# Second mixture of a three-stage kernel: each phase's compaction before its neighbours' counts, and its row transposes at a new place in TensorE's order

## The chip, the cores and the metric

The kernel runs on one core of a Trainium2 chip. The metric is the device time in microseconds (us) of one execution, as the median of the runs. In the text, PE is TensorE, DVE is VectorE, ACT is ScalarE, POOL is GpSimd and SP is SyncE.

## The reference

Three stages follow one another. The first is a recurrent attention over 4 batches, 8 heads and 768 steps. Its result, seen as 3072 tokens of 384 numbers, goes through a first mixture of 8 experts and then through a second. Only the second mixture is touched here:

```python
def _moe2_ref(x, w_gate, w1, w2):
    N, D = x.shape                      # 3072, 384
    E = w_gate.shape[1]                 # 8
    cap = N // E                        # 384
    flat = (x @ w_gate).flatten()
    order = np.argsort(-flat)
    assigned = -np.ones(N); counts = np.zeros(E)
    for idx in order:
        tok, e = int(idx) // E, int(idx) % E
        if assigned[tok] >= 0 or counts[e] >= cap:
            continue
        assigned[tok] = e; counts[e] += 1
    for e in range(E):
        mask = assigned == e
        out[mask] = np.maximum(x[mask] @ w1[e], 0.0) @ w2[e]
```

All pairs of token and expert are taken in falling order of their logit. A token goes to the first expert that still has room, and an expert is full at 384 tokens. So the experts fill up one after another, and each of them ends with exactly 384 tokens.

## The kernel before

The attention and the first mixture come first and end at about 539 us of the profiled execution. What follows is the second mixture, in 8 phases, one for each expert in the order in which they fill up. A phase p has these parts.

**The chain** (`chain(p)`) finds which expert fills up next and which tokens it gets. The key of every token is cut into three digits of 10 or 11 bits, and each digit is found in two levels. So a chain has six **counts**. In a count, DVE compares all keys with 46 thresholds (tile `cmp`), PE adds the results up in 12 products (L953, into `pcn`), DVE scales the sums (`xs`), PE adds over partitions (L960), DVE compares with what is still needed (`fl`), PE spreads that (L964), and DVE takes the maximum (`nn`), from which the next count's keys are made. After the sixth count come two more small products (L985 and L1018), and from them the list of free tokens for the next chain (`advance`). Phase 7 has no counts.

**The compaction** (`finish`, that is `place` and `compact`) turns the chosen tokens into a list of 384 row numbers: DVE compares in four parts (`oq`, L1077), PE makes 24 products (L1081, into `pcm`, in four parts of 6), DVE makes the indices `ix`, and POOL issues three indirect DMAs (the **gather**, L1094), each of which fetches 128 rows of the first mixture's output into `x2`.

**The transposes** (`tin`, L1134): for each of three column blocks kt, three products turn the rows (a = 0, 1, 2) into `pX`. ACT and DVE split that into a high and a low part (`x2h`, `x2l`). `pX` has two buffers, so the third block waits until the first has been split.

**The products** (`compute`): 72 products into `pH` (L518 to L520, the first matrix) and 72 into `pY` (the second), 144 a phase, each 128x384. `pH` has two buffers, each free once ACT (`h2h`) and DVE (`h2l`, L515) have read it. `pY` is written three times, for 128 tokens each; ACT scales it (`orow`, L1162) and POOL scatters it to the output (L1163).

**The weights** (`load2`): SP reads the number of the expert (`ei`) and loads four pieces of 768 KB into `stage`; ACT makes the high part `whi` (L1119) and DVE the low part `wlo` (L1120), in 16 pieces a phase.

A scheduler lays out one fixed order of instructions for each engine when the kernel is built. It takes the work in the order in which the code emits it, and what stands in `tc.high_priority(n)` counts as if it had been emitted n places earlier. `tc.issue_after(x)` keeps an instruction behind x in the order. At run time each engine takes its instructions in that order, and one that waits holds up all behind it on its engine. `compute(p)` yields 14 times, u counts the yields, and the loop over u emits the next phase's parts between the products: the chain of p + 1 and its compaction at u = 1 (`UC`), the weights at u = 3 and 11, the transposes at u = 11 (`UT`). The compaction of phases 2 to 7 has half the chain's priority, and the transposes are kept behind the product emitted last.

Of the kernel before, what the change touches and what calls it, by code (L numbers as in the profile page):

```python
# [28 lines left out]
E = 8  # L29
# [11 lines left out]
KS = 46  # L41
# [9 lines left out]
UC = 1  # L51
UT = 11
HC = 1000000
HP2 = HC // 2
HT = 1000
HL = 0
DEF = 2
# [11 lines left out]
H1 = 300  # L69
# [3 lines left out]
IT = 1  # L73
# [8 lines left out]
def tile_kernel(ctx: ExitStack, tc, rd, kd, wd, vd, ud, emb, tau, m1w1, m1w2, m1w2t, wg2, m2w1, m2w2, out):  # L82
    nc = tc.nc
# [11 lines left out]
    def bcast(ap, shape):  # L95
        return ap.to_broadcast(shape)
# [410 lines left out]
    pe = [None]  # L507

    def split_x(pX, n, hi, lo):
        nc.scalar.copy(hi, pX)  # L510
        nc.vector.tensor_sub(lo, pX, hi.bitcast(F32))
# [372 lines left out]
    with tc.tile_pool(name="m2", bufs=2) as mp, tc.tile_pool(name="ps2", bufs=2, space=PSUM) as ps:  # L884
# [4 lines left out]
        def small(shape, name, dt=F32, bufs=None):  # L889
            bufs = bufs or 1 + (name in twin)  # L890
            return ck.tile(shape, dt, name=name, bufs=bufs)

        plan = {}
        oqi = [None]
        pcm = ps.tile([128, 512], F32, name="pcm", bufs=1)

        def chain(p):
# [4 lines left out]
            if not last:  # L902
# [30 lines left out]
                for s in range(3):  # L933
                    for lv in range(2):
                        cmp = cmps[lv]
                        nq = 2 if p == 0 else NQ
                        hj = J // 2 // nq
                        w2 = w.rearrange("p (a b) -> p a b", b=2)
                        c4 = cmp[:, :J * KS].rearrange("p (a k b) -> p a k b", k=KS, b=2)
                        for q in range(nq):  # L940
                            js = slice(q * hj, (q + 1) * hj)
                            nc.vector.tensor_tensor(c4[:, js], bcast(w2[:, js, None, :], [128, hj, KS, 2]),
                                                    bcast((tblB if lv else tblA)[:, None], [128, hj, KS, 2]), op=ALU.is_ge)
                        if lv == 0:
                            w45 = small([128, J], "w45")
                            nc.vector.tensor_scalar(w45, w, float(KW), None, op0=ALU.add)
                            if s < 2:
                                big = small([128, J], "big")
                                nc.vector.scalar_tensor_tensor(big, w, SPLIT, dg[:, s + 1], op0=ALU.mult, op1=ALU.add)
                        o = 16 * lv  # L950
                        px = pcn[:, 48 + o:64 + o]
                        for a in range(J // 2):
                            nc.tensor.matmul(px, cmp[:, 2 * KS * a:2 * KS * a + 128],  # L953
                                             oh[:, 2 * a:2 * a + 2, :].rearrange("p b e -> p (b e)"),
                                             start=(a == 0), stop=(a == J // 2 - 1))
                        xs = small([128, 2, E], "xs", FP16)
                        nc.vector.tensor_tensor(xs, px.rearrange("p (b e) -> p b e", b=2), par16, op=ALU.mult)
                        pa = pcn[:, o:o + 8]
                        for b in range(2):
                            nc.tensor.matmul(pa[:, :E], psum2, xs[:, b], start=(b == 0), stop=(b == 1))  # L960
                        fl = small([KS, E], "fl", BF16)
                        nc.vector.tensor_tensor(fl, pa[:KS, :E], need[:KS], op=ALU.is_ge)
                        pb = pcn[:, o + 8:o + 16]
                        nc.tensor.matmul(pb[:, :E], ones[:KS, :], fl, start=True, stop=True)  # L964
                        nn = small([128, 1], "nn", bufs=4)
                        nc.vector.reduce_max(nn, pb[:, :E], axis=AX.X)
                        if lv == 0:
                            wn = small([128, J], "wb", FP16)
                            nc.vector.scalar_tensor_tensor(wn, bcast(nn, [128, J]), -float(KW), w45, op0=ALU.mult, op1=ALU.add)
                            w = wn  # L970
                            t1 = small([128, 1], "t1")
                            nc.vector.tensor_scalar(t1, nn, KW * SPLIT, -(KW + 1) * SPLIT, op0=ALU.mult, op1=ALU.add)
                        elif s < 2:
                            t4 = small([128, 1], "t4")
                            nc.vector.tensor_scalar(t4, nn, SPLIT, t1, op0=ALU.mult, op1=ALU.add)
                            wc = small([128, J], "wc")
                            nc.vector.tensor_scalar(wc, big, t4, SPLIT, op0=ALU.subtract, op1=ALU.min)
                            w = small([128, J], "w", FP16)
                            nc.vector.tensor_scalar(w, wc, -1.0, None, op0=ALU.max)
# [70 lines left out]
            def finish():  # L1050
                place()
                compact(p, slot)

            plan[p]["finish"] = finish
            if p == 0:
                with tc.high_priority(HC + 1000):
                    finish()
            if not last:
                advance()

# [65 lines left out]
        def tin(p):  # L1126
            d = plan[p]
            xh = d["xh"] = mp.tile([128, KT, CAP], F32R, name="x2h")
            xl = d["xl"] = mp.tile([128, KT, CAP], F32R, name="x2l")
            for kt in range(KT):  # L1130
                pX = ps.tile([128, CAP], F32, name="pX", bufs=2)
                for a in range(3):
                  with tc.issue_after(pe[0].ins) if IT and p else ExitStack():
                    nc.tensor.transpose(pX[:, a * 128:(a + 1) * 128], d["xr"][:, a, kt * 128:(kt + 1) * 128], ident)  # L1134
                split_x(pX, CAP, xh[:, kt, :], xl[:, kt, :])

# [33 lines left out]
        def hp(n, f, *a):  # L1170
            with tc.high_priority(n) if n else ExitStack():
                f(*a)

        hp(HC, chain, 0)
        load2(0, 0)
        if T0:
            hp(HC, tin, 0)
        if not UW:
            load2(0, 1)
        if not T0:  # L1180
            tin(0)
        for p in range(E):
            more = p + 1 < E
            for u, _ in enumerate(compute(p)):
                if UW and p == 0 and u == UW - 1:
                    load2(0, 1)
                if more:
                    if u == UC:
                        hp(H1 if p == 0 else HC, chain, p + 1)
                        hp(H1 if p == 0 else HP2, plan[p + 1]["finish"])  # L1190
                    if u == U0:
                        hp(HL, load2, p + 1, 0)
                    if u == U1:
                        hp(HL, load2, p + 1, 1)
                    if u == UT:
                        hp(HT, tin, p + 1)
# [51 lines left out]
```

## Time and profile before

| what | value |
|---|---|
| median of 3 runs | 855.87 us (852.36 to 856.16) |
| the profiled execution, its own time | 852.17 us |
| its span, first to last instruction | 850.4 us |
| mean granted clock of TensorE | 0.942 of full |
| busy in the span: PE, DVE, ACT, POOL | 776.8, 554.7, 319.9, 227.9 us |

The span is divided into stretches, and in each the profile gives the busy time of every engine and the clock that TensorE was granted, as a share of 2.4 GHz; there are two levels, 1.0 and 0.5. The work outside the span takes 852.17 - 850.4 = 1.8 us.

### The profile page before, as it was taken

What the parts mean: (1) busy time and instruction counts of PE and PEld (TensorE: products, weight loads), DVE (VectorE), ACT (ScalarE), POOL (GpSimd) and SP (SyncE); (2) the same over time, 40 slices, a digit from 0 to 9 for tenths busy, and PEclk for the clock granted to TensorE, in tenths of its full rate; (3) what the DMA queues carried; (4) which work ended last, traced back from release to release, by engine and by line L of the source; (5) the groups of instructions that cost most, each with busy time, mean ns of one, the idle gap of its engine ahead of it and who ended that gap; (6) DMA issues with size and microseconds to landing.
All of it is one profiled execution on the core that took longest, in us unless ns stands there. A gap on an engine that the chain in (4) does not pass through costs nothing.

```text
span 850.4 us, 14966 instructions
## 1 busy us (share of the span) xinstructions
PE 776.8 (91%) x5484; PEld 681.1 (80%) x5484; DVE 554.7 (65%) x1740; ACT 319.9 (38%) x763; POOL 227.9 (27%) x220
## 2 busy tenths in 40 slices
PE   5898998999989998999989999697979889899997
PEld 3787787888659897998989787485868778789997
DVE  9688899999534355344543546676878778787430
ACT  3334444443323454344443411423323323235431
POOL 4235477853200303203123002302021210112011
PEclk9799899999989999999999999787969979899999
DMA  8567457661253243433523002422323242426300
GB/s 277 167 193 247 137 185 249 189 202 39 66 181 116 102 149 100 158 114 106 184 88 105 5 1 84 150 87 100 124 72 140 80 154 94 145 69 223 122 29 29
DMA packets 39303, 107.66 MB, mean 127 GB/s; under 512 B 6666, under 2 KB 16700, under 8 KB 39228
## 3 DMA queue, kind: packets, MB, share of 16 engines
q1 hardware_dynamic: 32060, 87.71, 31.5%
q0 software_dynamic: 7168, 18.98, 6.3%
q8 instruction: 44, 0.72, 0.3%
q14 instruction: 31, 0.25, 0.1%
HBM read 87.16 MB, written 19.90 MB: 126 GB/s over the span
## 4 chain that ended last, share of the span: by engine, by line
PE 46%; issue 15%; DVE 4%; POOL 2%; DMA 1%; ACT 1%; another core or an unknown queue 1%; ACTq 0%; POOLq 0%; DVEq 0%
PE pY L520 7%; PE pY L518 7%; PE pY L519 6%; PE pH L518 6%; PE pH L519 6%; PE pH L520 6%; PE pO L657 2%; PE pcm L1081 1%; PE pcn L953 1%; DVE wlo L1120 1%; PE pX L624 1%; POOL x L1094 1%; POOL out_dram L1163 1%; PE pX L1134 1%
## 5 line engine op out<-in xcount | busy, mean ns | idle before, releaser
L515 DVE SCALAR_TENSOR_TENSOR hl<-pH,hh 128x416 fp32r<-128x416 f32 x64 | 37.6, 589 | 66.4 <-ACT hh L514 48.5
L518 PE MATMUL pH<-xhi,whi 128*128 128x416 f32 x192 | 72.1, 376 | 9.5 <-DVE hl L515 7.8
L1120 DVE TENSOR_TENSOR wlo<-stage,whi 128x384 fp32r<-128x384 f32 x128 | 68.3, 549 | 6.9 <-ACT whi L1119 6.8
L518 PE MATMUL pH<-x2h,whi 128*128 128x384 f32 x192 | 71.1, 371 | 1.8 <-DVE h2l L515 1.6
L734 POOL DMA_INDIRECT lg<-lr,ids x24 | 23.0, 959 | 179.6 <-DVE lr L659 173.2
L519 PE MATMUL pH<-x2l,whi 128*128 128x384 f32 x192 | 71.1, 371 | 0.0
L520 PE MATMUL pH<-x2h,wlo 128*128 128x384 f32 x192 | 70.1, 365 | 0.0
L1119 ACT CAST whi<-stage 128x384 fp32r<-128x384 f32 x128 | 57.0, 511 | 32.7 <-PE pH L519 19.3
L520 PE MATMUL pH<-xhi,wlo 128*128 128x416 f32 x192 | 69.0, 359 | 0.0
L519 PE MATMUL pH<-xlo,whi 128*128 128x416 f32 x192 | 68.6, 357 | 0.0
L518 PE MATMUL pY<-whi,h2h 128*128 128x384 f32 x192 | 67.7, 353 | 0.0
L520 PE MATMUL pY<-whi,h2l 128*128 128x384 f32 x192 | 67.7, 355 | 0.0
L1163 POOL DMA_INDIRECT out_dram<-orow,ix x24 | 24.3, 1015 | 159.3 <-ACT orow L1162 144.6
L519 PE MATMUL pY<-wlo,h2h 128*128 128x384 f32 x192 | 66.9, 350 | 0.0
L514 ACT ACTIVATE h2h<-pH 128x384 fp32r<-128x384 f32 x64 | 31.4, 490 | 93.8 <-PE pH L520 92.7
L188 DVE TENSOR_TENSOR wlo<-stage,whi 128x512 fp32r<-128x512 f32 x78 | 48.3, 684 | 24.8 <-ACT whi L187 24.8
L187 ACT CAST whi<-stage 128x512 fp32r<-128x512 f32 (+1 forms) x90 | 51.9, 647 | 31.5 <-PE pY L519 23.0
L520 PE MATMUL pY<-hh,wlo 128*128 128x416 f32 x168 | 60.5, 360 | 0.0
L518 PE MATMUL pY<-hh,whi 128*128 128x416 f32 x168 | 60.1, 359 | 0.0
L519 PE MATMUL pY<-hl,whi 128*128 128x416 f32 x168 | 59.1, 352 | 0.0
L350 PE MATMUL y<-vv,am 128*128 128x48 f32 x384 | 56.9, 273 | 0.0
L1094 POOL DMA_INDIRECT x<-y,ix x24 | 29.8, 1244 | 93.2 <-issue 52.4
(320 smaller groups left out, 1976.2 us busy)
## 6 DMA issues: line engine op xcount, KB each, us to landing
stage<-in_m1w_dram SPq DMA_DIRECT2D x32, 768.0 KB
stage<-in_m2w_dram SPq DMA_DIRECT2D x32, 768.0 KB
wz<-in_w_dram SPq DMA_DIRECT2D x24, 260.0 KB
rd<-in_r_dram SPq DMA_DIRECT2D x24, 256.0 KB
kd<-in_k_dram SPq DMA_DIRECT2D x24, 256.0 KB
xg<-zt SPq DMA_DIRECT2D x8, 627.2 KB
xr<-xg SPq DMA_DIRECT2D x24, 193.0 KB
vv<-in_v_dram SPq DMA_DIRECT2D x24, 192.0 KB
```

Source lines behind the costliest of these rows:

```text
L187: nc.scalar.copy(hi[:, s], t[:, o:o + g])
L188: (eng or nc.vector).tensor_tensor(lo[:, s], t[:, o:o + g], hi[:, s].bitcast(F32), op=ALU.subtract)
L350: yi = nc.tensor.matmul(y[:, o:o + D], ams[h][:, p, :], vv[:, 2 * p + h, :], start=(c == 0), stop=(c == 0 or h == 1))
L514: nc.scalar.activation(hi, pH, AF.Relu)
L515: nc.vector.scalar_tensor_tensor(lo, pH, 0.0, hi.bitcast(F32), op0=ALU.max, op1=ALU.subtract)
L518: nc.tensor.matmul(o, wh, xh, start=start, stop=False)
L519: nc.tensor.matmul(o, wh, xl, start=False, stop=False)
L520: pe[0] = nc.tensor.matmul(o, wl, xh, start=False, stop=stop)
L1094: gi = nc.gpsimd.indirect_dma_start(out=xr[:, a, :], out_offset=None, in_=y1, in_offset=bass.IndirectOffsetOnAxis(ap=ix[:, a:a + 1], axis=0))
L1119: nc.scalar.copy(hi[:, c], t[:, r * g:r * g + g])
L1120: (nc.vector if e == "v" else nc.gpsimd).tensor_tensor(lo[:, c], t[:, r * g:r * g + g], hi[:, c].bitcast(F32), op=ALU.subtract)
L1163: s_ = nc.gpsimd.indirect_dma_start(out=out, out_offset=bass.IndirectOffsetOnAxis(ap=d["ix"][:, a:a + 1], axis=0), in_=orow, in_offset=None)
```

## The change

The compaction of every phase gets a priority just above that of the chains (`HF`), where it had a lower one. For phases 0 to 2 (`LEAD`) it stays at the place u = 1 or before the loop; for phases 3 to 7 it is emitted at u = 5 (`UF`) without a priority. The chains are emitted one phase earlier: chain 1 before phase 0's transposes with priority 300, and chain p + 2 at u = 11 of phase p. The transposes of phases 0 to 2 are kept behind the fourth count (`CR`) of the next chain, and those of later phases behind the product emitted last, as before.

The diff:

```diff
--- before.py
+++ after.py
@@ -51,7 +51,11 @@
 UC = 1
 UT = 11
 HC = 1000000
-HP2 = HC // 2
+HF = 1000
+HL1 = 300
+LEAD = 3
+CR = 3
+UF = 5
 HT = 1000
 HL = 0
 DEF = 2
@@ -892,6 +896,7 @@
 
         plan = {}
         oqi = [None]
+        counts = {}
         pcm = ps.tile([128, 512], F32, name="pcm", bufs=1)
 
         def chain(p):
@@ -950,9 +955,10 @@
                         o = 16 * lv
                         px = pcn[:, 48 + o:64 + o]
                         for a in range(J // 2):
-                            nc.tensor.matmul(px, cmp[:, 2 * KS * a:2 * KS * a + 128],
+                            ci = nc.tensor.matmul(px, cmp[:, 2 * KS * a:2 * KS * a + 128],
                                              oh[:, 2 * a:2 * a + 2, :].rearrange("p b e -> p (b e)"),
                                              start=(a == 0), stop=(a == J // 2 - 1))
+                        counts.setdefault(p, []).append(ci)
                         xs = small([128, 2, E], "xs", FP16)
                         nc.vector.tensor_tensor(xs, px.rearrange("p (b e) -> p b e", b=2), par16, op=ALU.mult)
                         pa = pcn[:, o:o + 8]
@@ -1052,9 +1058,6 @@
                 compact(p, slot)
 
             plan[p]["finish"] = finish
-            if p == 0:
-                with tc.high_priority(HC + 1000):
-                    finish()
             if not last:
                 advance()
 
@@ -1130,7 +1133,7 @@
             for kt in range(KT):
                 pX = ps.tile([128, CAP], F32, name="pX", bufs=2)
                 for a in range(3):
-                  with tc.issue_after(pe[0].ins) if IT and p else ExitStack():
+                  with tc.issue_after(counts[p + 1][CR].ins if p < LEAD else pe[0].ins):
                     nc.tensor.transpose(pX[:, a * 128:(a + 1) * 128], d["xr"][:, a, kt * 128:(kt + 1) * 128], ident)
                 split_x(pX, CAP, xh[:, kt, :], xl[:, kt, :])
 
@@ -1172,11 +1175,13 @@
                 f(*a)
 
         hp(HC, chain, 0)
+        hp(HC + HF, plan[0]["finish"])
         load2(0, 0)
         if T0:
             hp(HC, tin, 0)
         if not UW:
             load2(0, 1)
+        hp(HL1, chain, 1)
         if not T0:
             tin(0)
         for p in range(E):
@@ -1185,9 +1190,10 @@
                 if UW and p == 0 and u == UW - 1:
                     load2(0, 1)
                 if more:
-                    if u == UC:
-                        hp(H1 if p == 0 else HC, chain, p + 1)
-                        hp(H1 if p == 0 else HP2, plan[p + 1]["finish"])
+                    if u == (UC if p + 1 < LEAD else UF):
+                        hp(HC + HF if p + 1 < LEAD else 0, plan[p + 1]["finish"])
+                    if u == UT and p + 2 < E:
+                        hp(HC, chain, p + 2)
                     if u == U0:
                         hp(HL, load2, p + 1, 0)
                     if u == U1:
```

What this does to the engines' orders is shown at three places. The line numbers shift: L953, L960 and L964 become L958, L966 and L970, L1081 becomes L1084, L1094 L1097, L1134 L1137, L1163 L1166, and L518 to L520 become L522 to L524.

The first place is PE around the transposes of phase 1. The `pcm` row is the last product of phase 1's compaction, `oh2` marks a count of chain 2, and `pY` rows are products of phase 0. Before:

```order
L1081 MATMUL pcm_5910<-vv2_6553,oq_6555 128x15
L519 MATMUL pY_6737<-wlo_6234,h2h_6705 128x384
...
L953 MATMUL pcn_3080<-oh2_6887,cmp1_3343 128x16
...
L960 MATMUL pcn_3080<-xs_6932,psum2_3339 128x8
...
L964 MATMUL pcn_3080<-fl_6936,ones_83 128x8
L1134 MATMUL pX_6780<-ident_73,x2_6590 128x128
L1134 MATMUL pX_6786<-ident_73,x2_6590 128x128
```

The same place in the change:

```order
L1084 MATMUL pcm_5910<-vv2_6553,oq_6555 128x15
L523 MATMUL pY_6737<-wlo_6234,h2h_6618 128x384
...
L966 MATMUL pcn_3080<-xs_6799,psum2_3339 128x8
...
L966 MATMUL pcn_3080<-xs_6825,psum2_3339 128x8
L524 MATMUL pY_6709<-whi_6233,h2l_6692 128x384
...
L522 MATMUL pY_7045<-whi_6233,h2h_6523 128x384
...
L524 MATMUL pY_7045<-whi_6233,h2l_6706 128x384
...
L1137 MATMUL pX_7018<-ident_73,x2_6590 128x128 x3
```

Before, one product and one count stood between the last compaction product and the first transpose; now 42 products and four counts do.

The second place is PE around the transposes of phase 3 in the change; phases 4 and 5 look the same. `pY_8165` is the third block of phase 2's second matrix.

```order
L1084 MATMUL pcm_5910<-vv2_7760,oq_7762 128x15
L522 MATMUL pY_7857<-whi_7554,h2h_7825 128x384
L523 MATMUL pY_7857<-wlo_7555,h2h_7825 128x384
L524 MATMUL pY_7829<-whi_7554,h2l_7826 128x384
...
L524 MATMUL pY_8165<-whi_7554,h2l_7745 128x384
L1137 MATMUL pX_8138<-ident_73,x2_7797 128x128
L1137 MATMUL pX_8144<-ident_73,x2_7797 128x128
L522 MATMUL pY_8165<-whi_7554,h2h_7811 128x384
...
L1137 MATMUL pX_8138<-ident_73,x2_7797 128x128
```

And before:

```order
L1081 MATMUL pcm_5910<-vv2_7673,oq_7675 128x15
...
L964 MATMUL pcn_3080<-fl_8056,ones_83 128x8
...
L518 MATMUL pH_7787<-x2h_7338,whi_7191 128x384
...
L518 MATMUL pH_7815<-x2h_7338,whi_7191 128x384
...
L520 MATMUL pY_7857<-whi_7316,h2l_7798 128x384
L1134 MATMUL pX_7900<-ident_73,x2_7710 128x128 x3
```

Before, 51 products and three counts stood between the last compaction product and the first transpose of phase 3; now it is 22 products and no whole count.

The third place is POOL around the gather of phase 3. `orow_7854` is the first block of phase 2's result. Before:

```order
L1163 DMA out_0_dram<-orow_7392,ix_6586 3072x384
L1094 DMA x2_7710<-y1_67,ix_7706 128x384 x3
L1163 DMA out_0_dram<-orow_7854,ix_7146 3072x384
L1163 DMA out_0_dram<-orow_7924,ix_7146 3072x384
L1163 DMA out_0_dram<-orow_7952,ix_7146 3072x384
```

In the change:

```order
L1166 DMA out_0_dram<-orow_7630,ix_6586 3072x384
L1166 DMA out_0_dram<-orow_7854,ix_7146 3072x384
L1097 DMA x2_7797<-y1_67,ix_7793 128x384 x3
L1166 DMA out_0_dram<-orow_8162,ix_7146 3072x384
L1166 DMA out_0_dram<-orow_8190,ix_7146 3072x384
```

The first scatter of the phase now stands ahead of the next phase's gather, and it is the same for the gathers of phases 4 and 5.

## Rows read from the trace of the kernel before

**Rows 1.** Windows: stretch, length, busy and count of PE, PEld, DVE, ACT, POOL; clock, DMA.

```profile
551.15:756.97 205.82, 184.74 (x1368) 159.95 (x1369) 157.65 (x690) 66.95 (x148) 32.41 (x28) 0.88 0.31 107
787.50:813.91 26.41, 26.41 (x155) 25.78 (x153) 13.46 (x27) 13.27 (x30) 2.89 (x3) 1.00 0.26 91
581.46:594.81 13.35, 7.28 (x52) 5.51 (x51) 7.21 (x26) 2.75 (x7) 5.59 (x4) 0.62 0.36 119
621.57:635.86 14.29, 9.75 (x58) 8.28 (x58) 10.02 (x36) 3.02 (x7) 3.88 (x3) 0.52 0.30 97
663.47:670.00 6.53, 4.41 (x27) 3.60 (x27) 4.91 (x17) 0.07 (x1) 1.57 (x2) 0.74 0.54 201
687.01:700.74 13.73, 9.83 (x74) 8.60 (x73) 10.72 (x37) 1.93 (x5) 3.24 (x3) 0.63 0.32 102
731.68:741.78 10.10, 7.64 (x37) 6.73 (x37) 7.69 (x24) 2.23 (x5) 0.98 (x2) 0.66 0.61 209
```

**Rows 2.** Groups of PE, 551 to 757 us: line, tiles, shapes, count, busy, mean, idle before.

```profile
L519 PE MATMUL pH<-x2l,whi 128*128 128x384 f32 x120 | 46.9, 391 | 0.0
...
L520 PE MATMUL pY<-whi,h2l 128*128 128x384 f32 x110 | 39.8, 366 | 0.0
...
L953 PE MATMUL pcn<-oh,cmp 128*128 128x16 bf16 x396 | 15.4, 171 | 9.7 <-DVE cmp L942 8.7 <-DVE oh L932 0.8
L1081 PE MATMUL pcm<-vv,oq 128*128 128x15 bf16 x120 | 11.7, 218 | 1.9 <-DVE oq L1077 1.7
L1134 PE MATMUL pX<-ident,x 128*128 128x128 f32 x42 | 9.7, 351 | 5.5 <-DMA x<-y,ix 5.5
```

**Rows 3.** Timeline of PE before and in phase 1's transposes: start, length, [idle <- releaser].

```profile
581.02 0.59 PE L1081 MATMUL pcm<-vv,oq 128*128 128x15 bf16 x6
...
588.01 1.09 PE L1134 MATMUL pX<-ident,x 128*128 128x128 f32 x4 [4.72 <-DMA x<-y,ix]
...
590.02 0.69 PE L1134 MATMUL pX<-ident,x 128*128 128x128 f32 x2 [0.60 <-DMA x<-y,ix]
...
592.00 0.52 PE L520 MATMUL pY<-whi,h2l 128*128 128x384 f32 x1
...
595.54 0.34 PE L520 MATMUL pY<-whi,h2l 128*128 128x384 f32 x1
595.71 0.34 PE L518 MATMUL pY<-whi,h2h 128*128 128x384 f32 x1
```

**Rows 4.** Timeline of POOL, the gathers of phases 0 and 1 and a scatter.

```profile
548.07 0.95 POOL L1094 DMA_INDIRECT x<-y,ix  x1 [0.30 <-issue]
582.74 1.08 POOL L1094 DMA_INDIRECT x<-y,ix  x1 [33.72 <-DVE gg L1088]
...
585.79 2.14 POOL L1094 DMA_INDIRECT x<-y,ix  x1 [0.30 <-issue]
590.32 1.00 POOL L1163 DMA_INDIRECT out_dram<-orow,ix  x1 [2.38 <-ACT orow L1162]
```

**Rows 5.** Timeline of PE, phase 0's last transposes before its products.

```profile
551.15 0.69 PE L1134 MATMUL pX<-ident,x 128*128 128x128 f32 x2 [0.21 <-DMA x<-y,ix]
```

**Rows 6.** Timeline of PE, two counts of chain 3 without products between them.

```profile
624.20 0.49 PE L953 MATMUL pcn<-oh,cmp 128*128 128x16 bf16 x12 [2.45 <-DVE cmp L942]
624.95 0.19 PE L960 MATMUL pcn<-xs,psum 128*128 128x8 f16 x2 [0.27 <-DVE xs L957]
625.48 0.16 PE L964 MATMUL pcn<-fl,ones 46*128 46x8 bf16 x1 [0.34 <-DVE fl L962]
627.13 0.69 PE L518 MATMUL pH<-x2h,whi 128*128 128x384 f32 x1 [1.48 <-DVE h2l L515]
```

**Rows 7.** Timeline of PE, a count of a later chain that waits for DVE.

```profile
734.49 0.47 PE L953 MATMUL pcn<-oh,cmp 128*128 128x16 bf16 x12 [2.11 <-DVE cmp L942]
```

**Rows 8.** Timeline of DVE: one comparison of a count, one piece of low weights.

```profile
579.82 0.73 DVE L942 TENSOR_TENSOR cmp<-wb,tblB 128x1104 bf16<-128x1104 f16 x1
...
581.73 0.55 DVE L1120 TENSOR_TENSOR wlo<-stage,whi 128x384 fp32r<-128x384 f32 x1
```

**Rows 9.** Timeline of ACT: one block of the output scaled.

```profile
595.52 0.58 ACT L1162 ACTIVATE orow<-pY,gg 128x384 f32<-128x384 f32 x1
```

## The prediction

> **What bounds the kernel now.** I read the windows first, because the change moves work only inside the second mixture. The reader should see there how much of a phase is waiting. A phase without counts, from one phase's transposes to the next, takes 26.4 us at full clock [rows 1]; it holds 144 products at 0.17 us each [rows 3] and 9 transposes. From the last transposes of phase 0 to those of phase 5 the kernel takes 205.8 us at a mean clock of 0.88 [rows 1]. The work in that stretch I add up from the groups of PE [rows 2]: six groups of products like the two shown, 3 x 120 + 3 x 110 = 690, at 0.174 us make 120; 33 counts (396 / 12) at about 0.5 us make 16; 5 compactions (120 / 24) at 1.6 us make 8; 42 transposes at 0.12 us make 5; the small products at a chain's end make 2. That is 151 us. So some 55 of 206 us are waits and half clock, and the change can only win or lose there.
>
> Where the 55 us lie is the second question, and the timeline of PE answers it. It shows five places where PE waits and the clock then stands at half for some us. For each place I take the window's length and subtract the work found in it [rows 1].
> - Phase 1's transposes, 581.5 to 594.8: PE waits 4.72 us for the gathered rows [rows 3], then works at half clock (a product shows 0.52 us, and 0.34 us at full clock). 13.4 us hold 10 products, 9 transposes and two counts, 3.8 us of work: 9.6 lost.
> - Phase 2's start, 621.6 to 635.9: two counts follow each other with no products between, and PE waits 2.45, 0.27, 0.34 and 1.48 us [rows 6]. 14.3 us hold about 20 products, 6 transposes and two counts, 5.2 us: 9.1 lost.
> - Three places in later chains, where a count waits 2.1 us for DVE (one is shown [rows 7], the others are alike) and half clock follows. Their windows of 6.5, 13.7 and 10.1 us hold about 11, 19 and 21 products besides counts and a compaction, 2.4 + 5.9 + 4.2 us: 17.8 lost.
>
> That is 36.5 us. The other 18 are waits of a few tenths at single counts, and phase 0's slow start.
>
> **The change, part by part.** The number of instructions of each kind stays the same, so only waits change. T is the end of a compaction's last product.
>
> *How late the gather is.* In phase 1, T is 581.6 (581.02 + 0.59) [rows 3]. The first gather DMA starts at 582.7, the third at 585.8 [rows 4]: 1.1 us after T, then 1.5 us apart. The rows are there when the transposes start, at 588.0 and 590.0, that is 5.3 and 4.2 us after their DMA's start; in phase 0 the last of them came 3.1 us after its start at 548.07 [rows 4, 5]. So a gather's first row block lands 4.2 to 6.4 us after T and its last 7 to 8.4 us after it.
>
> *Phase 0.* Its rows land at 551.15 whatever PE does before [rows 5]. The third and fourth count of chain 1 now run in that wait. But all six transposes of the first two blocks, instead of two, come after it: 4 x 0.24 us at half clock, less a count's 0.5 that is out of the way. I take +0.4, between 0 and +1.
>
> *Phase 1.* Between T and the first transpose stand 42 products (7.3 us) and four counts (2 us), more than the 8.4 us the rows need. So the wait of 4.72 us goes, and with it the half clock: -9.6. What is late next is the chain. From one count to the next DVE has `fl`, `nn`, a comparison of 0.73 us and up to four pieces of `wlo` at 0.55 us [rows 8], some 3.5 us; between the first two counts PE has only 9 products, 1.6 us. For the four counts I add up 1.7 + 0.7 + 0.3 + 0.3 = 3.0 us of waiting. The transposes then stand alone ahead of phase 1's first products, which need ACT's and DVE's split: about 1.0 us. Half clock may follow once in four: 0.6. Together +4.6 (2 to 9). Net -5.0.
>
> *Phase 2.* Right behind the compaction stand 2 products, then two whole counts, then `pH` products that need DVE's `h2l`, which itself stands behind the second count. That is the pattern of [rows 6], and I give it the same price: 9.1 lost before and after, net 0 (-4 to +2).
>
> *Phases 3, 4 and 5.* No two counts stand together any more; at least 13 products (2.3 us) stand between them. I take the three places off: -17.8. What comes in is a wait for the gather. POOL must first issue the scatter of `orow`, whose `pY` ends 3 products after T: 0.5 us, then ACT 0.58 us [rows 9] and some 0.3 us of hand-over, then 1.0 us on POOL and a gap of 0.3 [rows 4]. So the gather starts at T + 2.7 and its first block lands at T + 5.8 with the 3.1 us of phase 0 (T + 8 with the 5.3 of phase 1). PE comes to the transposes after 22 products and two waits for the chain, at T + 4.3. I take 1.5 us of waiting for the first block (0 to 3.7), 0.5 and 0.8 for the next two, 0.3 for the third column block and 0.9 for the last products of the chain, which now have only 11 products between them: 4.0. Half clock after it costs 2.5 us where it comes; I give it 0.6. Sum 5.5 a phase, +16.5. Net -1.3, between -10 and +11.
>
> *Phase 6.* Before, its transposes (787.5) waited for nothing, and the clock was full from there on [rows 1]. Now 23 products (4 us) stand between the compaction and them: about 2 us of waiting and 0.3 x 2.5 of half clock, +2.8. *Phase 7* has 60 products in between, 10.4 us, which hide its gather of at most 8.4: nothing. SP's order differs only at phase 7's expert number, which is read after phase 6's last load and not among them; the load behind it waits for a free `stage` buffer as before, so I put it at nothing, and at the 1 us of a late first piece if that cover is gone.
>
> *The tenths.* Of the 18 us of small waits some 5 should go, since a wait of PE for DVE is covered wherever products stand between a count's steps, and phases 3 to 5 now have more there: I take -2, between -6 and 0.
>
> The sum is 0.4 - 5.0 + 0 - 1.3 + 2.8 - 2 = -5.1 us. Against the profile's own 852.2 us this gives 847. That execution lies at the low end of the runs (852.4 to 856.2, median 855.9), so for the median I add half the distance: 848.5 us, 0.9% below the median. A change under 0.5%, 4.3 us, could not be told from none.
>
> **Rivals.**
>
> *A. The gathers are covered (841 us).* If the clock stays up in phases 3 to 6 and the first block lands at T + 4.3 as in a gather that waits for no scatter, the four phases lose some 2 us less each: 8 us. For it speaks that phases 6 and 7 of before had their transposes among products at full clock [rows 1]; against it, the scatter ahead of the gather.
>
> *B. The waits only change places (855 us).* Phase 1's wait may come back whole as waits of the chain with half clock: [rows 6] show that two counts without products cost 9.1 us. Then the -5.0 is 0 and the tenths stay, and the time is that of before less 1 or 2 us. For it speaks that the chain is a string of PE and DVE steps which neither version shortens; against it, that 9 products stand between the two counts, where [rows 6] have none.
>
> *C. Half clock at four phase starts (867 us, slower).* In phases 3 to 6 PE reaches the transposes too early. Between the last block of products before them and the first after them lie some 6 us with about 8 products, the rest waits, a count and transposes. In phase 1 of before the same mix (a wait for the gather, transposes, a count) was followed by half clock until 594.8 and cost 9.6 us in all [rows 1, 3]. At that price the four phases cost 4 x 9.6 = 38.4 in place of my 16.5 + 2.8, 19 us more: 867. It decides from about 9 us a place. For it speaks the place before the gather of POOL's scatter; against it, that the wait I count is 1.5 us and not 4.72. The Trainium skill (TensorE: Matmul & The Clock Gate, Part 4: PE-mode transpose) says that transposes do not count as a busy TensorE in the way that products do, which would let the clock fall at these places. The trace does not settle it: where transposes stood among products, at 787.5, the clock held [rows 1], and where it fell there was a wait as well.
>
> *That the change does nothing* is excluded, since the orders differ at every phase.
>
> **How the numbers follow.** The forecast, 843 to 853.5, gets 0.45, of which 0.33 is faster by over 0.5% (below 851.6) and 0.12 is within it. A gets 0.19, all faster; B 0.18, all within; C 0.18, of which 0.17 slower. So faster 0.52, same 0.30, slower 0.18. The range for 8 in 10 takes in A's half with the lesser gain, B, and C's milder half: 838 to 862.
>
> **What would show it.** Phase 1's first transpose should not wait for the gather, and the clock should be full there. Phase 2's start should still show waits of about 2 us at a count and a stretch at half clock. The transposes of phases 3, 4, 5 and 6 should each wait 1 to 2 us for the gathered rows, with a scatter on POOL just ahead of the gather. The waits of 2.1 us for DVE's comparison should be gone from phases 3 to 5. The prediction is wrong if half clock follows at most of these four places (C), if phase 1 loses over 8 us (B), or if phase 2's start is covered as well, which would make it faster than I say.

## The result, and the profile after

The changed kernel is slower: the ratio of its time to that of before is **1.0058, 95% interval 1.0034 to 1.0082**, with medians of 857.9 us (20 runs) and 854.0 us (20 runs of before, measured beside it). The ratio is that of the means over the runs within 1.5% of the fastest (19 and 18 of the 20), and so not the quotient of these medians. The forecast was 848.5 us with 0.52 for faster; the time lies inside the range of 838 to 862, and the sign is wrong. The profiled execution took 865.6 us (span 863.9), of which 8 us arose ahead of the change: its first compaction started at 547.7 us, that of before at 539.6. The 3524 TensorE instructions that the traces show up to there stand in the same order in both, and in the eleven profiles below this start lies between 524 and 546 us. So the traces are compared from the first compaction's start to the start of the last product: 311.0 us (547.68 to 858.63), and 305.5 us before (539.62 to 845.16).

The windows of the changed kernel, at the places that [rows 1] show of before (stretch, length, busy time and count of PE, PEld, DVE, ACT and POOL, granted clock, DMA share, GB/s): phase 1's transposes, phase 2's start, the transposes of phases 3, 4, 5 and 6, and the stretch from there to phase 7's.

```profile
588.40:602.40 14.00, 11.51 (x95) 8.99 (x95) 11.87 (x41) 4.80 (x10) 5.03 (x5) 1.00 0.41 142
620.00:636.00 16.00, 10.26 (x93) 8.63 (x93) 12.75 (x47) 3.02 (x8) 3.33 (x3) 0.68 0.28 88
675.40:684.70 9.30, 5.98 (x41) 4.84 (x40) 3.53 (x13) 1.92 (x4) 4.97 (x5) 0.82 0.28 85
715.70:727.00 11.30, 8.90 (x57) 6.91 (x55) 4.34 (x14) 1.92 (x4) 4.00 (x4) 0.70 0.28 88
756.95:768.50 11.55, 8.30 (x55) 6.51 (x55) 4.33 (x14) 1.92 (x4) 3.99 (x4) 0.70 0.26 85
791.00:804.50 13.50, 7.92 (x36) 6.85 (x35) 5.28 (x14) 1.92 (x4) 3.51 (x4) 0.75 0.50 183
804.50:827.40 22.90, 22.90 (x146) 22.43 (x145) 12.11 (x27) 11.45 (x26) 4.86 (x5) 1.00 0.24 76
```

Phase 1's transposes, at a clock of 0.62 before, now have 1.00. That is so in this execution: in a second profile of the same kernel (experiment 9) the same stretch shows 0.88, with half clock behind a count's wait of 1.44 us, and still no wait for rows:

```profile
565.07:579.07 14.00, 12.40 (x93) 10.31 (x94) 10.69 (x36) 4.80 (x10) 4.09 (x5) 0.88 0.33 126
```

Phase 2's start still waits and still falls to half clock. The four lines after it are new places of half clock, and the last of them, phase 6, stands where before had 26.4 us without any wait.

The timeline of PE at these places of the changed kernel (start, length, instruction, and in brackets the idle time and its releaser):

```profile
590.20 0.46 PE L958 MATMUL pcn<-oh,cmp 128*128 128x16 bf16 x12 [1.45 <-DVE cmp L947]
...
599.30 0.53 PE L1137 MATMUL pX<-ident,x 128*128 128x128 f32 x3
...
625.54 0.48 PE L958 MATMUL pcn<-oh,cmp 128*128 128x16 bf16 x12 [2.12 <-DVE cmp L947]
...
679.08 0.66 PE L1137 MATMUL pX<-ident,x 128*128 128x128 f32 x2 [3.32 <-DMA x<-y,ix]
...
689.07 0.44 PE L522 MATMUL pH<-x2h,whi 128*128 128x384 f32 x1 [0.36 <-DVE h2l L519]
...
758.33 0.41 PE L1137 MATMUL pX<-ident,x 128*128 128x128 f32 x2 [1.02 <-DMA x<-y,ix]
...
760.16 0.44 PE L1137 MATMUL pX<-ident,x 128*128 128x128 f32 x2 [0.78 <-DMA x<-y,ix]
...
762.23 0.69 PE L1137 MATMUL pX<-ident,x 128*128 128x128 f32 x2 [1.45 <-DMA x<-y,ix]
...
794.39 0.41 PE L1137 MATMUL pX<-ident,x 128*128 128x128 f32 x2 [3.00 <-DMA x<-y,ix]
796.75 0.69 PE L1137 MATMUL pX<-ident,x 128*128 128x128 f32 x2 [1.94 <-DMA x<-y,ix]
...
798.72 0.69 PE L1137 MATMUL pX<-ident,x 128*128 128x128 f32 x2 [0.64 <-DMA x<-y,ix]
...
799.84 0.52 PE L523 MATMUL pY<-wlo,h2h 128*128 128x384 f32 x1
```

Phase 4's three waits (717.33 to 720.14) are 1.26, 0.53 and 0.60 us. A product shows 0.52 us at 799.84, as in phase 1 of before [rows 3]: half clock.

The timeline of POOL at phase 5's and phase 6's gathers:

```profile
753.77 0.96 POOL L1166 DMA_INDIRECT out_dram<-orow,ix  x1 [29.79 <-ACT orow L1165]
755.04 1.17 POOL L1097 DMA_INDIRECT x<-y,ix  x1 [0.30 <-issue]
756.51 1.50 POOL L1097 DMA_INDIRECT x<-y,ix  x1 [0.30 <-issue]
758.32 0.95 POOL L1097 DMA_INDIRECT x<-y,ix  x1 [0.30 <-issue]
...
788.83 1.08 POOL L1097 DMA_INDIRECT x<-y,ix  x1 [22.76 <-PE pY L524]
790.21 1.09 POOL L1097 DMA_INDIRECT x<-y,ix  x1 [0.30 <-issue]
791.61 1.00 POOL L1097 DMA_INDIRECT x<-y,ix  x1 [0.30 <-issue]
```

Phase 5's row blocks are there 3.3, 3.7 and 3.9 us after their DMA's start (758.33 - 755.04, and so on), phase 6's 5.6, 6.5 and 7.1 us after it, though no scatter stands ahead of them. Before, POOL issued the gathers of phases 6 and 7 long ahead of their use, phase 6's from 762.81 (transposes at 787.50) and phase 7's from 769.40 (transposes at 813.91):

```profile
762.81 0.98 POOL L1094 DMA_INDIRECT x<-y,ix  x1 [1.48 <-PE pX L1134]
...
769.40 1.22 POOL L1094 DMA_INDIRECT x<-y,ix  x1 [0.30 <-PE pH L520]
```

**A ledger of the second mixture**, made as the prediction made its places: the length of each stretch less the work in it (a product 0.174 us, a count's twelve rows 0.31, a compaction 1.76, a transpose 0.118, other small products 0.06).

| place | lost before, us | lost after | forecast of the difference | measured |
|---|---|---|---|---|
| phase 0 | 13.9 | 13.7 | +0.4 | -0.2 |
| phase 1's transposes | 9.6 | 4.7 | -5.0 | -4.9 |
| phase 2's start | 9.3 | 8.6 | 0 | -0.7 |
| phases 3 to 5: three waits in chains, now three gathers | 18.7 | 18.1 | -1.3 | -0.6 |
| phase 6's transposes | 0 | 8.1 | +2.8 | +8.1 |
| the stretches between these places | 12.8 | 16.8 | -2 | +4.0 |
| phase 7 to the end | 0.4 | 0.3 | 0 | -0.1 |
| sum | 64.7 | 70.3 | -5.1 | +5.6 |

The sum meets the 5.4 us by which the second mixture took longer. Two rows of the table are off, by 5.3 and 6.0 us, and together they make the whole error of 10.7 us; the other rows cancel to within 0.6.

Lost time in this ledger is not only waiting. In the stretches between the places PE stands idle for 1.7 us before and for 2.6 us after (length less PE's busy time); the rest of the 12.8 and 16.8 us is work that took longer than the prices.

### The profile page after: what moved, and what is told of

It is laid out like the page before. It is cut to its first block, busy times and chain, and to the rows that moved or that the text cites. A ratio compares the mean times of both kernels' runs of the same rounds, so it can differ in the third digit from the quotient of the medians.

```text
span 863.9 us, 14971 instructions
## 1 busy us (share of the span) xinstructions
PE 785.2 (91%) x5484; PEld 682.8 (79%) x5484; DVE 555.0 (64%) x1740; ACT 319.4 (37%) x763; POOL 226.2 (26%) x220
## 4 chain that ended last, share of the span: by engine, by line
PE 36%; issue 23%; POOL 4%; DVE 4%; DMA 3%; ACT 1%; another core or an unknown queue 1%; POOLq 0%; ACTq 0%; SPq 0%; DVEq 0%
PE pY L524 5%; PE pH L522 5%; PE pY L522 5%; PE pH L524 5%; PE pY L523 5%; PE pH L523 5%; POOL x L1097 2%; DMA x<-y,ix 2%; PE pO L661 1%; POOL out_dram L1166 1%; PE pcm L1084 1%; PE pcn L958 1%; DVE wlo L1123 1%; PE pX L1137 1%; PE pX L628 1%
## 5 line engine op out<-in xcount | busy, mean ns | idle before, releaser
L522 PE MATMUL pH<-xhi,whi 128*128 128x416 f32 x192 | 72.8, 380 | 10.7 <-DVE hl L519 10.3
L522 PE MATMUL pH<-x2h,whi 128*128 128x384 f32 x192 | 69.5, 367 | 2.4 <-DVE h2l L519 2.4
L524 PE MATMUL pH<-xhi,wlo 128*128 128x416 f32 x192 | 69.7, 363 | 0.0
L522 PE MATMUL pY<-whi,h2h 128*128 128x384 f32 x192 | 68.4, 356 | 1.2 <-ACT orow L1165 1.0
L524 PE MATMUL pY<-whi,h2l 128*128 128x384 f32 x192 | 68.7, 361 | 0.3 <-DVE h2l L519 0.3
L523 PE MATMUL pH<-x2l,whi 128*128 128x384 f32 x192 | 68.9, 360 | 0.0
L524 PE MATMUL pH<-x2h,wlo 128*128 128x384 f32 x192 | 68.9, 361 | 0.0
L1166 POOL DMA_INDIRECT out_dram<-orow,ix x24 | 25.2, 1049 | 164.7 <-ACT orow L1165 122.5
L518 ACT ACTIVATE h2h<-pH 128x384 fp32r<-128x384 f32 x64 | 31.3, 489 | 92.2 <-PE pH L524 72.3
L524 PE MATMUL pY<-hh,wlo 128*128 128x416 f32 x168 | 60.5, 360 | 0.0
L522 PE MATMUL pY<-hh,whi 128*128 128x416 f32 x168 | 60.1, 359 | 0.0
L354 PE MATMUL y<-vv,am 128*128 128x48 f32 x384 | 59.0, 280 | 0.0
L354 PEld LDWEIGHTS y<-vv,am 128*128 128x128 f32 x384 | 54.4, 205 | 0.2
```

The costliest lines, as they stand in the source:

```text
L354: yi = nc.tensor.matmul(y[:, o:o + D], ams[h][:, p, :], vv[:, 2 * p + h, :], start=(c == 0), stop=(c == 0 or h == 1))
L518: nc.scalar.activation(hi, pH, AF.Relu)
L522: nc.tensor.matmul(o, wh, xh, start=start, stop=False)
L523: nc.tensor.matmul(o, wh, xl, start=False, stop=False)
L524: pe[0] = nc.tensor.matmul(o, wl, xh, start=False, stop=stop)
L1166: s_ = nc.gpsimd.indirect_dma_start(out=out, out_offset=bass.IndirectOffsetOnAxis(ap=d["ix"][:, a:a + 1], axis=0), in_=orow, in_offset=None)
```

## The experiments

**Theory L:** the loss comes from phases 3 to 6, where too few products stand between a compaction and its transposes: the gathered rows are late, and half clock follows. Its rivals: E, the early part loses; K, chains that are written a phase ahead cost, wherever the gather stands; H, transposes at a phase start bring half clock by themselves. All ratios are to runs of the kernel before on the same chip.

| kernel | ratio to before, 95% interval | second mixture in the trace, us |
|---|---|---|
| before | 1 | 305.5 |
| changed | 1.0058 (1.0034 to 1.0082) | 311.0 |
| changed, second measurement | 1.0123 (1.0082 to 1.0164) | 312.1 |
| early part alone | 0.9963 (0.9927 to 1.0000) | 299.9 |
| late part alone | 1.0158 (1.0108 to 1.0209) | 320.3 |
| place 2 | 0.9862 (0.9810 to 0.9914) | 293.5 |
| compaction first everywhere | 0.9935 (0.9901 to 0.9968) | 297.1 |
| phases 6 and 7 alone at place 2 | 1.0014 (0.9979 to 1.0048) | 300.5 |
| the same, second measurement | 1.0015 (0.9988 to 1.0042) | 301.4 |
| early scheme for two phases, place 2 | 0.9827 (0.9767 to 0.9887) | 289.3 |
| rows before weights in phase 6 | 1.0005 (0.9960 to 1.0050) | 310.6 |
| filler ahead of phase 6's transposes | 1.0100 (1.0065 to 1.0135) | 307.1 |
| early scheme for two phases, place 1 | 0.9787 (0.9745 to 0.9829) | 289.2 |

**1 and 2. The two halves of the change.** The first kernel has the order of before from phase 3 on, except that chain 3 stays early, since phase 2's transposes are kept behind it. The second is the reverse. The edit of the first:

```
-                    if u == (UC if p + 1 < LEAD else UF):
-                        hp(HC + HF if p + 1 < LEAD else 0, plan[p + 1]["finish"])
-                    if u == UT and p + 2 < E:
+                    if u == UC:
+                        if p + 1 < LEAD:
+                            hp(HC + HF, plan[p + 1]["finish"])
+                        else:
+                            if p + 1 > LEAD:
+                                hp(HC, chain, p + 1)
+                            hp(HC // 2, plan[p + 1]["finish"])
+                    if u == UT and p + 2 <= LEAD:
                         hp(HC, chain, p + 2)
```

> Phases 0 to 2 as in the changed kernel, from phase 3 on the chain, compaction and transposes where the kernel before has them. Theory L (the loss comes from phases 3 to 6, whose transposes wait for late gathered rows and then run at half clock): the first three phases keep their gain, so 854 - 6 = 848 us, ratio to before about 0.993. Theory E (the early part loses, for instance by chains written a phase ahead): no better than before, 854 to 858.

> Phases 0 to 2 as before, from phase 3 on the fixed place of the changed kernel. Theory L: by the lost time added up after phase 2's transposes (39.2 us in the changed kernel, 28.4 before) about 854 + 11 = 865 us, ratio 1.013, with waits for gathered rows of 1 to 3 us at the transposes of phases 3 to 6. Theory E: near 854.

Early alone: 0.9963, which is 3 us of gain by the times and 5.6 us by the trace. Late alone: 1.0158, 13.5 us slower. E is out: by itself the early part is no slower (its interval ends at 1.0000), and the late part is. The halves don't add up exactly, since with the early scheme gone phase 2's transposes too came close behind their compaction (a wait of 1.69 us).

**3. Place 2 for the later compactions.**

```
-UF = 5
+UF = 2
```

> The changed kernel with the compactions of phases 3 to 7 three blocks earlier, so that 40 to 100 products stand between them and their transposes in place of 20 to 26. Chains stay where the changed kernel has them. Theory L: the waits for gathered rows of 1 to 3.3 us go and so does the half clock behind them; of 31.6 us lost at four places some 10 to 15 stay in waits of the chains, so about 858 - 17 = 841 us, ratio to before 0.985. Rival H (the half clock comes from the transposes and counts at a phase start, the wait for the gather is a side matter): the waits go, 10 us, but half clock stays, and the time is 848 to 850. Rival K (the chains written a phase ahead cost, not the place of the gather): no change, 858.

0.9862, 12 us faster than before. By the trace 32 to 87 products now stand between these compactions and their transposes. No transpose of phases 3 to 7 waits for rows any more. The windows of this kernel that begin at the transposes of phases 4, 5 and 6:

```profile
714.60:724.00 9.40, 9.40 (x57) 8.89 (x57) 8.57 (x54) 5.18 (x12) 3.30 (x3) 1.00 0.60 203
751.50:762.00 10.50, 10.50 (x65) 10.09 (x65) 9.72 (x48) 6.08 (x15) 2.97 (x3) 1.00 0.79 239
780.00:790.00 10.00, 10.00 (x60) 9.38 (x58) 3.83 (x8) 5.10 (x12) 2.35 (x3) 1.00 0.51 183
```

PE is busy throughout at full clock, with nine transposes in each. So K is out (the chains stand where the changed kernel has them), and H too. What is left from phase 2 on is in the chains, 11 us ahead of phase 2's and of phase 3's transposes and 5.7 ahead of the next two.

**4. Compaction first in every phase.**

```
-                    if u == (UC if p + 1 < LEAD else UF):
-                        hp(HC + HF if p + 1 < LEAD else 0, plan[p + 1]["finish"])
+                    if u == UC:
+                        hp(HC + HF, plan[p + 1]["finish"])
...
-                  with tc.issue_after(counts[p + 1][CR].ins if p < LEAD else pe[0].ins):
+                  with tc.issue_after(counts[p + 1][CR].ins if p < E - 2 else pe[0].ins):
```

> Compaction first and transposes behind the fourth count in every phase but the last two, whose transposes stand at the usual place, compactions one after the other in phase 5 and 6. Theory L: no gather is late, each of phases 3 to 5 pays waits of the chain as in phase 1 of the changed kernel (some 4 us), so about 842 us, ratio 0.986. Rival H: each phase start keeps half clock, 850. Rival K: 858.

0.9935: no rows are late, but more stays in the chains than I expected. By its time alone this could be the 850 us of rival H. The trace decides against it: the transposes of phases 3 to 5 run at full clock, and half clock stands at the counts behind the compactions. The counts behind the compactions of phases 3, 4 and 5 each wait 2.0 us for DVE, and two of the compactions themselves 1.0 and 1.7 us. Phase 4's:

```profile
686.11 2.17 PE L1084 MATMUL pcm<-vv,oq 128*128 128x15 bf16 x24 [1.68 <-DVE oq L1080]
...
690.32 0.47 PE L958 MATMUL pcn<-oh,cmp 128*128 128x16 bf16 x12 [2.04 <-DVE oh L937]
```

**5, 9 and 10. Phase 6 by itself, and the changed kernel beside it.** `UF` becomes 2 from phase 6 on alone, 53 products in place of 23.

```
-                    if u == (UC if p + 1 < LEAD else UF):
+                    if u == (UC if p + 1 < LEAD else UF if p + 1 < 6 else 2):
```

> The changed kernel with only the compactions of phases 6 and 7 three blocks earlier: 53 products instead of 23 between phase 6's compaction and its transposes. Theory L: the 8.4 us that I read at phase 6's transposes go, 858 - 8 = 850 us, ratio to before 0.995. Rival S (phase 6 cost the 2.8 us of the prediction, the rest lies in phases 3 to 5): 855.

> The kernel with only phases 6 and 7 moved, once more beside the changed kernel. By its trace (theory L) 8 to 9 us below the changed kernel, ratio to before about 0.997; if only half of that is real, 4 us below it, ratio 1.001.

> The changed kernel once more, beside the next one on the same chip, since the time of the kernel with phase 6 alone moved (855.4, ratio 1.001) gave back half of the 8.9 us that its trace showed. Either reading: ratio to before 1.004 to 1.008. In the trace the second mixture should again take about 311 us from its first compaction's start, with waits for gathered rows at the transposes of phases 3 to 6 and a granted clock near 0.75 behind them.

The first measurement (855.4 us, ratio 1.0014) showed half of what its trace did, but the changed kernel had been timed apart from it. Beside each other on one chip they took 846.0 and 837.7 us: 8.3 us, where the ledger has 8.1. The traces agree to about 1 us: from phase 5's first transposes to the last product the changed kernel took 100.3 and 99.3 us in its two profiles, this one 91.4 and 91.8. The whole second mixture differs by more (10.5 and 10.6 us), since ahead of that point, where nothing was changed, half clock lasted less long at phase 4. In the second profile one row block of phase 6 still came 0.5 us late. On that chip all three kernels were 12 to 18 us faster, before too (835.9). For the two that were profiled there the traces show that this lies ahead of the second mixture, which starts at 524 us and whose 312.1 and 301.4 us repeat the earlier 311.0 and 300.5. Before was not profiled there, so it stays open why the changed kernel is 10 us behind it on this chip and 4 to 5 us on the first, and why the kernel with phase 6 moved, 4 to 5 us ahead of before by the traces, is not ahead of it by the times.

**7. Why phase 6's rows were later than the others'.** Phase 6's second weight load waits for its gather (`GD` is 0, so no load had such a wait):

```
-                if GD and p == 0 and i == 1:
+                if p == 6 and i == 1:
```

> The changed kernel with one added wait: the second weight load of phase 6 starts only when phase 6's gathered rows are there. Theory W (the rows of phase 6 come 5.6 to 7.1 us after their DMA's start, and not 3.3 to 3.9 as in phases 4 and 5, because weights stream at the same time): they come 3.3 to 4 us after it, the waits of 3.0, 1.9 and 0.6 us shrink to about 2 us in all, and the kernel gains 3 to 4 us, 854. Rival N: the rows are as late as before, 858.

This kernel's timelines of POOL and of PE in phase 6:

```profile
783.02 1.30 POOL L1097 DMA_INDIRECT x<-y,ix  x1 [21.34 <-PE pY L523]
784.62 1.22 POOL L1097 DMA_INDIRECT x<-y,ix  x1 [0.30 <-issue]
786.15 0.94 POOL L1097 DMA_INDIRECT x<-y,ix  x1 [0.30 <-issue]
```

```profile
786.58 0.30 PE L1137 MATMUL pX<-ident,x 128*128 128x128 f32 x1 [0.72 <-DMA x<-y,ix]
787.92 0.55 PE L1137 MATMUL pX<-ident,x 128*128 128x128 f32 x3 [1.05 <-DMA x<-y,ix]
789.20 0.44 PE L1137 MATMUL pX<-ident,x 128*128 128x128 f32 x2 [0.73 <-DMA x<-y,ix]
```

The rows come 3.6, 3.3 and 3.1 us after their DMA's start, and the waits fall from 5.6 to 2.5 us: theory W. While the gather was under way the DMA engines were busy for 0.38 of the time here, and for 0.70 in the changed kernel:

```profile
783.00:789.20 6.20, 3.70 (x22) 2.99 (x20) 2.49 (x5) 0.58 (x1) 4.46 (x4) 1.00 0.38 112
788.80:798.70 9.90, 4.33 (x21) 3.30 (x20) 4.36 (x13) 0.89 (x2) 4.36 (x4) 0.81 0.70 238
```

The Trainium skill (DMA: Bandwidth & Descriptors, "Queues, rings and completion order") says that each DMA engine takes turns, packet by packet, between the queues that have work for it. The trace agrees as far as it goes: the rows' blocks take about twice as long beside the weights; the turns themselves it does not show. The order behind phase 6 also moved in this kernel, so its time (1.0005) is not laid to the wait alone. From phase 5's first transposes to the last product it took 95.6 us, the changed kernel 100.3 and 99.3. That the whole second mixture is no shorter (310.6 us) lies ahead of that point, which took 215.0 us here and 210.6 and 212.8 there, with the same order and more half clock.

**8. Work in place of the wait.** 36 products whose result goes nowhere, between phase 6's compaction and its transposes (nothing of the output is left out):

```
+FN = 36
...
+            if p == 6:
+                ww = plan[5]["w", 1][0]
+                for q in range(FN):
+                    nc.tensor.matmul(pcm[:, 64:448], ww[:, :128], ww[:, 128:512], start=True, stop=True)
```

> The changed kernel with 36 added products (6.3 us) into an unused part of a PSUM bank between phase 6's compaction and its transposes; their result goes nowhere. Theory I (half clock follows the idle wait, not the transposes): the wait of 5.6 us is filled, the clock stays at 1.0 through the transposes and the products behind them, and the 2.8 us of half clock are saved: 858 + 0.7 - 2.8 = 856 us. Rival H (transposes at a phase start bring half clock by themselves): the granted clock falls all the same, and the time is 859.

The filler, then PE at the transposes, then the windows of the filler, of the transposes and of what follows:

```profile
773.13 6.40 PE L1137 MATMUL pcm<-whi 128*128 128x384 f32 x36
...
782.73 0.38 PE L1142 MATMUL pX<-ident,x 128*128 128x128 f32 x2
783.55 0.66 PE L1142 MATMUL pX<-ident,x 128*128 128x128 f32 x4 [0.44 <-DMA x<-y,ix]
```

```profile
773.10:782.70 9.60, 9.60 (x57) 9.60 (x56) 6.83 (x20) 0.58 (x1) 4.17 (x4) 1.00 0.65 231
782.70:787.00 4.30, 3.86 (x25) 3.31 (x24) 1.58 (x3) 1.83 (x4) 0.13 (x1) 1.00 0.09 33
787.00:797.00 10.00, 10.00 (x57) 9.69 (x57) 5.35 (x11) 5.56 (x13) 1.80 (x2) 1.00 0.35 120
```

The clock stays at 1.00 (0.75 in the changed kernel). The same transposes, at the same place, bring no half clock when PE works instead of waiting: theory I. From phase 5's first transposes to the last product it took 97.5 us, against 100.3 and 99.3 in the changed kernel's two profiles: about the 2.1 us expected. The times don't show it: 1.0100 (1.0065 to 1.0135), no better than the changed kernel. So the clock's part rests on the trace.

**6 and 11. A faster version.** Early scheme for phases 0 and 1 alone (`LEAD = 2`), place 2, and then place 1:

```
-LEAD = 3
+LEAD = 2
-UF = 5
+UF = 2
```

> The better of the kernels so far (place 2) with the early scheme for phases 0 and 1 alone, so that phase 2's compaction too stands at the fixed place. By the order phase 3's counts get 7 to 17 products between them instead of 4, phase 2's stay close together. If a count without products ahead of it is what the phases 2 and 3 still pay (11 us each before their transposes), phase 3 falls to the 5.7 us of phases 4 and 5: 846 - 5 = 841 us, ratio to before 0.980. If it does not matter, 846 and 0.986.

> The fastest kernel so far (early scheme for phases 0 and 1, place 2 from phase 2 on) with place 1 instead of 2: 65 to 75 products between compaction and transposes in place of 52 to 56. Theory L: the rows were there already, so nothing is left to gain: 838 to 840 us, ratio 0.983. If an earlier compaction still helped, below 835; if its four large DVE steps now stand in the way of the blocks' splits, 843.

0.9827 and 0.9787, with 289.3 and 289.2 us in the trace: equal within the error. Once the rows are there, an earlier compaction gains nothing. Phase 3 fell to 5.7 us, as expected. Phase 2's start still waits for DVE three times:

```profile
616.02 0.59 PE L1084 MATMUL pcm<-vv,oq 128*128 128x15 bf16 x6 [1.42 <-DVE oq L1080]
...
621.12 0.49 PE L958 MATMUL pcn<-oh,cmp 128*128 128x16 bf16 x12 [1.93 <-DVE cmp L947]
...
624.03 0.69 PE L522 MATMUL pH<-x2h,whi 128*128 128x384 f32 x1 [1.47 <-DVE h2l L519]
```

These two beat both kernels, by about 2% against before, and the second by 3% against the changed one (818.9 and 846.0 us on one chip).

## Why the prediction was wrong

Step by step, as it put them:

- **Phase 0 and phase 1: right.** Phase 1's transposes wait for no rows, and -5.0 was -4.9. The first wait of its counts, 1.45 us, is the one that I sized at 1.7. The half clock that I gave one chance in four stayed away in this execution, which is partly luck: eleven profiles have this early part and this wait, and half clock followed it in nine, among them the second profile of the changed kernel.
- **Phase 2: right.** Net 0 was -0.7; the waits of about 2 us and the half clock are there.
- **Phases 3, 4 and 5: right in size, but by luck: two errors cancel.** The 2.1 us waits in chains are gone. The gather starts at T + 2.8 in phase 5 (compaction's end 752.2, DMA 755.04), behind a scatter; I said T + 2.7. The waits of 1.5, 0.5 and 0.8 us were 1.0, 0.8 and 1.5 in phase 5, 1.3, 0.5 and 0.6 in phase 4, and a single one of 3.3 in phase 3, where POOL's first gather instruction took 2.65 us instead of 1.2. Half clock was too cheap: I gave it 0.6 of 2.5 us, and it came at all three places. Besides the waits 2.0, 3.8 and 3.4 us were lost there, most of it at half clock; I had 1.5 for these, and 1.2 for the third column block and the chain's last products, which show no wait of their own.
- **Phase 6: the first step that failed.** "About 2 us of waiting and 0.3 x 2.5 of half clock" was 5.6 us of waiting and 2.5 of half clock: 8.1 instead of 2.8. The wait is longer because weights stream beside the gather (experiment 7): the first block landed 7.1 us after the compaction's end and the last 11.4, where I had 4.2 to 6.4 and at most 8.4. The half clock comes with the wait, since it stays away when work fills it (experiment 8). The 5.3 us in phase 1 of before, against 3.1 in phase 0 [rows 3 to 5], were the warning; I took the difference as spread. The share of 0.36 in [rows 1] hides the reason, since it is the mean of a longer stretch. While that first block was under way the share was 0.67:

```profile
582.74:588.01 5.27, 0.16 (x1) 0.03 (x1) 4.37 (x15) 0.00 (x0) 4.59 (x3) 0.68 0.67 224
```

  Of all places this was also the one where before paid nothing.
- **The tenths: the second step that failed.** I took -2, since a count that waits for DVE is covered by products; it was +4.0. The premise was wrong first: the waits of a few tenths at single counts, of which some 5 us should go, are not there. In these stretches before stands idle for 1.7 us in all, half of it one wait of 0.83 us. The counts' waits did go, but DVE then does a chain's steps in one run, and the split of a block's output that PE needs next comes behind them. At 689.07 PE waits 0.36 us for `h2l`, which DVE starts only after 16 small steps of the chain, from 686.62 on:

```profile
686.62 0.17 DVE L972 TENSOR_REDUCE nn<-pcn 128x1 f32<-128x8 f32 x1 [0.41 <-PE pcn L970]
...
688.47 0.54 DVE L519 SCALAR_TENSOR_TENSOR h2l<-pH,h2h 128x384 fp32r<-128x384 f32 x1
```

  Seven such waits of 0.26 to 0.46 us for `h2l` or `orow`, 2.6 us in all, stand between products after, and none so long in these stretches before. So idle time rose by 0.9 us; the other 3.1 of the 4.0 are work that took longer than the ledger's prices, and their cause stays open.
- **The rivals.** C had the mechanism nearest to what happened, at 9.6 us a place; the four places cost 5.4, 6.2, 6.6 and 8.1. What decided it was the wait, as in its price, and not the transposes: by the rule that it cited (the Trainium skill, TensorE: Matmul & The Clock Gate, "Part 4: PE-mode transpose") the clock could have fallen at transposes anywhere, and in experiments 3 and 8 it stayed at 1.00 through them, with products around them.
- **Two slips that decide nothing.** Half the distance to the median is 1.8 us, which makes the forecast 848.9 and not 848.5, and by their own shares the chances are 0.31 for same and 0.17 for slower.

With phase 6 repaired the change is worth nothing that the times show (1.0014, 1.0015), and with phases 3 to 5 repaired too it gains 1.4% (experiment 3).

## What to carry to other kernels

When a load is moved closer to its use, count the work that stands between them, in products, and compare it with the longest flight that the trace shows for such a load, not with the shortest; and look at the DMA share of that stretch, since bulk transfers beside it lengthen the flight. A place where the kernel before waits for nothing is where such a move can only lose: price it first. The waits of 2.4 to 5.6 us at these four places were paid twice, once as idle time and once as 2 to 4 us lost besides, most of it at half clock. So covering such a wait whole is worth more than shortening it: in experiment 7, with 2.5 us of waiting left in phase 6, half clock still followed.

## What the runs showed of the hardware

- The same 192 KB row block of a gather came 3.1 to 3.9 us after its DMA's start with the DMA engines at a share of 0.38 to 0.44 (experiment 7, phase 5 of the changed kernel), and 5.6 to 7.1 us at 0.70. In experiment 8, also at 0.70, one block took 8.1. The first block of phase 3 took 4.9 at 0.32; there POOL's own instruction took 2.65 us, elsewhere 0.9 to 1.5.
- The loss besides the waits did not grow with them: 2.4 us of waiting in phase 4 came with 3.8 us of it, 5.6 us in phase 6 with 2.5. Nor does a short wait always bring half clock: the 1.45 us at phase 1's count did in nine profiles and not in two, and in experiment 3 waits of 0.7 to 1.2 us for `h2l` among products did not.
- The changed kernel's median was 857.9 us in one measurement and 846.0 in another, 1.4% apart, while its second mixture took 311.0 and 312.1 us in the two profiles. Only comparisons on one chip could carry the 1% at issue.
